# Attention, expert layer and feed-forward on one core: queries and keys laid nine tokens to a partition, second expert weights two rows to a partition

## The chip, the cores and the metric

One core of a Trainium2 chip runs the whole program in one launch. The metric is the device time of one execution in microseconds (us), the median of several executions.

## The reference, cut to what matters

Four batches of eight heads, 576 tokens, head size 64. Each head has a downsampled attention (means of four tokens) and a local one (tokens closer than four). The result, 2304 rows of 512, goes through a soft mixture of eight experts with four slots each and then through a feed-forward block with a squared relu.

```python
q_d = q.reshape(B, H, 144, 4, D).mean(axis=3)          # the same for k and v
out_up = np.repeat(sm_attn(q_d, k_d, v_d), 4, axis=2)
mask = np.abs(pos[:, None] - pos[None, :]) < 4
out_local = softmax(where(mask, q @ k.T / 8, -1e9)) @ v
x = (out_up + out_local) -> [2304, 512]
logits = x @ phi;  slot_input = softmax(logits, 0).T @ x
slot_out[e] = relu(slot_input[e] @ w1[e]) @ w2[e]      # 8 experts, 512 -> 1024 -> 512
y = softmax(logits, 1) @ slot_out
out = relu(y @ w_in) ** 2 @ w_out                      # 512 -> 2048 -> 512
```

## The kernel before, in words

The attention goes over 16 units, a unit being two heads of one batch (u = 0 to 15, four units a batch). The two heads lie on partitions 0 to 63 and 64 to 127 of most tiles. The order of all work is written out by hand: START for the first three units, then for every s from 3 to 15 the letters of ORDER, then DRAIN. Each letter is one function for one unit; in step s the letter T transposes unit s, S and s make the scores of unit s-1, p and q transpose the probabilities of unit s-2, and V, D, A and t make the values, their sum and the token rows of unit s-3. All engines take their instructions in that order.

Loads go through one queue, SP's, which issues them in the order of the program. A step loads queries and keys of unit s+2 (Q, `load_qk`, L343), two windowed loads of v for unit s-1 (L, `load_v`, L360, pieces of 64 numbers), v once more in groups of eight tokens for the downsampled path (4, `load_v4`, L374), and two or three pieces of 512 KB of the weights (l, `load_next`, L152, L155, L158; LOADN = [2, 2, 3] * 6 says how many, 2.33 on average). Queries and keys have two tiles each, so the load of unit s+2 waits for the transposes of unit s. The weight pieces lie in a ring of tiles that come free as the experts use them.

A load of queries or keys of a unit brings [2 heads, 576 tokens, 64]. Before the change a partition of 96 holds, for each head and each third of the tokens, two neighbouring tokens side by side, 128 numbers: six pieces of 512 B a partition. `transposes` (L377 to L392) turns it into [64 per head, tokens]: for each of q and k and each head, three transposes of [96, 128] into one PSUM tile "tr" [128, 3, 96] (L384). The even tokens then lie on its partitions 0 to 63 and the odd ones on 64 to 127, and two copies of 64x288 put them into every second column of `qs` or `kzs` (L390 ACT for q; L392 ACT for k of head 0, DVE for k of head 1). "tr" has three buffers in rotation, so the fourth group, k of head 1, waits for the two copies of the first.

What follows uses `qs` and `kzs` in token order: `downsample` on POOL (L400, L402), `scores_local` (L408, L414), `scores_down` (L438). `value_sums` (POOL, L482) and `value_sums2` (DVE, L488) add up v for the downsampled path, `values_down` (L523) multiplies with it. At the end of each batch `stage_g2` and `stage_g3` (L609 to L632) collect the slots' inputs.

The experts: `expert_up` (L824) multiplies with w1 into a tile with hidden columns 256g to 256g+255 on partitions 32g and up, `expert_mid` transposes that in two halves (L836), `expert_down` (L848) takes chunk by chunk of w2. A piece of w2 is [128, 2, 512], rows 256j + 128t + p before the change: two runs of 2 KB a partition. The feed-forward block (L909 to L1032) follows, 96 steps of nine 128x512 matmuls each.

Of the kernel before, what the change touches and what calls it, by code (L numbers as in the profile page):

```python
# [9 lines left out]
F32 = mybir.dt.float32  # L10
# [8 lines left out]
B, H, S, D = 4, 8, 576, 64  # L19
# [50 lines left out]
def attention_moe_ffn_kernel(  # L70
# [12 lines left out]
    nc = tc.nc  # L83
    cp = ctx.enter_context(tc.tile_pool(name="const", bufs=1))
    ring = ctx.enter_context(tc.tile_pool(name="ring", bufs=1))
# [5 lines left out]
    def bank(tag, shape, bufs, name, dt=F32):  # L91
        return ps.tile(shape, dt, tag=tag, bufs=bufs, name=name)

    def bt(shape, name):
        return bank("t", shape, 3, name)
# [4 lines left out]
    ident = cp.tile([128, 128], F32, name="ident")  # L100
# [5 lines left out]
    for g in range(4):  # L106
        r = slice(32 * g, 32 * g + 32)
# [34 lines left out]
    def load(kind, i, j, place):  # L142
        pool, tag = where[kind, i, j] = place
        name = f"{kind}{i}_{j}"
        if kind in ("win", "wout"):

            t = pool.tile([128, 512, 2], I32, tag=tag, name=name)
            if kind == "win":
                src = w_in.bitcast(I32).rearrange("(t p) f -> p t f", t=4)[:, i, 1024 * j:1024 * j + 1024]
            else:  # L150
                src = w_out.bitcast(I32)[128 * i:128 * i + 128]
            nc.sync.dma_start(out=t.rearrange("p f w -> p (f w)"), in_=src)  # L152
        elif kind == "w1":
            t = pool.tile([128, FE], F32, tag=tag, name=name)
            nc.sync.dma_start(out=t, in_=w1[i].rearrange("(p t) f -> p t f", t=4)[:, j])  # L155
        else:
            t = pool.tile([128, 2, DM], F32, tag=tag, name=name)
            nc.sync.dma_start(out=t, in_=w2[i].rearrange("(t p) f -> p t f", t=8)[:, 2 * j:2 * j + 2])  # L158
        got[kind, i, j] = t

    def load_next(n=1):
        for _ in range(n):
            if not loads or not free:
                return
            kind, i, j = loads[0]

            fits = [x for x in free if x[0] is not wa or kind in ("w1", "w2") and i == 0 and int(x[1][1:]) >= WRES]
            fits.sort(key=lambda x: x[0] is not wa)
            if kind == "wout" or kind == "win" and (LPOS[4 * j + i] > 50 or lb is None) or kind != "win" and i == NE - 1:
                fits = [x for x in free if x[0] is ring]  # L170
            elif kind != "win" and i >= LBE + 1:
                fits = [x for x in fits if x[1][0] != "b"]
                fits.sort(key=lambda x: x[0] is ring)

            if any(j > 1 and (j, i // 2) not in win for k, i, j in got if k == "win") and kind != "win":
                if sum(x[0] is ring for x in free) < 2:
                    fits = [x for x in fits if x[0] is not ring]
            if not fits:
                return
            place = fits[0]  # L180
            free.remove(place)
            loads.popleft()
            load(kind, i, j, place)
# [11 lines left out]
    for g in range(4):  # L195
        m = maskf[32 * g:32 * g + 32]
# [97 lines left out]
    with tc.tile_pool(name="att", bufs=1, side="right") as ap:  # L294
        NV = 2
        vws, qs, kzs = [], [], []
        for i in range(NV):

            t = ap.tile([128, NB, D], F32, name=f"vw{i}")
# [3 lines left out]
        for i in range(2):  # L303
            t = aq.tile([128, SP + 6], F32, name=f"q{i}")
# [4 lines left out]
            t = aq.tile([128, 2, SP + 6], F32, name=f"kz{i}")  # L309
# [25 lines left out]
        def load_qk(u):  # L335
            b, hp = divmod(u, NP)
            h0 = 2 * hp
            st = U[u]
            for nm, src in (("q", q), ("k", k)):

                t = ring.tile([128, 1024], F32, tag=f"{nm}{u % 2}", name=f"{nm}{u}")[0:96, 0:768]
                t = t.rearrange("p (h a c) -> p h a c", h=2, a=3)
                nc.sync.dma_start(out=t, in_=src[b, h0:h0 + 2].rearrange("h (a p r) d -> p h a (r d)", a=3, r=2))  # L343
                st[nm] = t

        def load_v(u):
# [30 lines left out]
        def transposes(u):  # L377
            st = U[u]
            for j, nm in enumerate("qk"):
                for h in range(2):  # L380

                    t = bt([128, 3, 96], f"tr{u}_{j}{h}")
                    for i in range(3):
                        nc.tensor.transpose(t[:, i], st[nm][:, h, i], ident[0:96, 0:96])  # L384
                    hr = slice(64 * h, 64 * h + 64)
                    to = (kzs[u % 2][hr, h] if j else qs[u % 2][hr])[:, 3:3 + S].rearrange("p (i c r) -> p i c r", i=3, r=2)
                    for r in range(2):
                        o, i_ = to[:, :, :, r], t[64 * r:64 * r + 64]
                        if not j:
                            nc.scalar.mul(out=o, in_=i_, mul=1.0 / 128.0)  # L390
                        else:
                            (nc.vector.tensor_copy if h else nc.scalar.copy)(out=o, in_=i_)  # L392
# [258 lines left out]
        def gate_rows(b):  # L651
# [6 lines left out]
            else:  # L658
# [8 lines left out]
                nc.vector.tensor_tensor(out=ctt_lo, in0=m, in1=ctt_hi, op=ALU.subtract)  # L667

        load_qk(0)
        for x in LOADS.split():  # L670
            if x[0] == "l":
                load_next(int(x[1:]))
            elif x == "phi":
                nc.sync.dma_start(out=phis, in_=phi.rearrange("(c p) s -> p c s", p=128))
            else:
                dict(Q=load_qk, L=load_v)[x[0]](int(x[1:])) if x[0] != "4" else load_v4(int(x[1:]))
# [3 lines left out]
        tm.enter_context(tc.manual_schedule())  # L680
        step = {
            "V": values, "T": transposes, "D": values_down, "A": value_adds, "Q": load_qk,
            "L": load_v, "S": scores_local, "p": probs_local, "E": exp_local, "s": scores_down, "d": downsample,
            "v": value_sums, "m": max_down, "q": probs_down, "e": exp_down, "n": norm_local, "N": norm_down,
# [52 lines left out]
        t = bt([1, 128], "mtp")  # L737
# [4 lines left out]
        t = bt([128, 2], "mbp")  # L742
# [23 lines left out]
        t = bt([128, 4, 32], "stp")  # L766
# [47 lines left out]
    for i in range(2):  # L814
        t = xp.tile([128, 2, 4, NS], F32, name=f"ht{i}")
# [3 lines left out]
    def expert_up(e):  # L819

        t = bank(("s", "sd")[e % 2], [128, 256], 1, f"hp{e}")
        for kt in range(4):
            for g in range(4):
                nc.tensor.matmul(  # L824
                    t[32 * g:32 * g + 32], sT[:, kt], got["w1", e, kt][:, 256 * g:256 * g + 256],
                    start=(kt == 0), stop=(kt == 3), tile_position=(0, 32 * g), skip_group_check=True,
                )
            done("w1", e, kt)
        hs = xp.tile([128, 256], F32, tag="hs", bufs=2, name=f"hs{e}")
        nc.scalar.activation(out=hs, in_=t, func=AF.Relu)  # L830
        return hs

    def expert_mid(e, hs):
        t = bt([128, 2, 4, NS], f"htp{e}")
        for i in range(2):
            nc.tensor.transpose(t[:, i].rearrange("p g s -> p (g s)"), hs[:, 128 * i:128 * i + 128], ident)  # L836

        ht = hts[e % 2]
        if e >= 2:
            nc.gpsimd.memset(ht[:, :, :, 4 * e - 8:4 * e - 4], 0.0)  # L840
        nc.scalar.copy(out=ht[:, :, :, 4 * e:4 * e + 4], in_=t[:, :, :, 4 * e:4 * e + 4])
        return ht
# [20 lines left out]
    hs = expert_up(0)  # L863
    for e in range(NE):
        if e == 0:
            hs, hs1 = expert_up(1), hs
            ht = expert_mid(0, hs1)
        else:
            ht = expert_mid(e, hs)
            if e + 1 < NE:  # L870
                hs = expert_up(e + 1)
# [165 lines left out]
    for i in range(2, len(steps) + LOOK):  # L1037
        up = lambda name, shape: pf.tile(shape, F32, tag="up", bufs=2, name=name)
        for x in SLOTS.get(i, ()):
            j = int(x[1:])  # L1040
# [6 lines left out]
        if i < len(steps):  # L1047
            c, f = steps[i]
# [43 lines left out]
```

## Time and profile before

| | us |
|---|---|
| three timed executions | 459.60, 465.48, 466.72 |
| their median | 465.48 |
| span of the profiled execution | 462.2 |

The span is from the first to the last instruction in one execution, 3.3 us less than the median of the timed ones; a time of its own is not recorded for the profiled execution. It falls into attention (to about 185 us), experts (to about 223), and the feed-forward block. PE is TensorE, with PEld its weight loads; DVE, ACT, POOL and SP are the other engines; PEclk and "clock" are the granted TensorE clock as a share of 2.4 GHz (0.5 is 1.2 GHz). The rows of the trace stand in a section of their own below.

### The profile page before, as it was taken

What the parts mean: (1) busy time and instruction counts of PE and PEld (TensorE: products, weight loads), DVE (VectorE), ACT (ScalarE), POOL (GpSimd) and SP (SyncE); (2) the same over time, 40 slices, a digit from 0 to 9 for tenths busy, and PEclk for the clock granted to TensorE, in tenths of its full rate; (3) what the DMA queues carried; (4) which work ended last, traced back from release to release, by engine and by line L of the source; (5) the groups of instructions that cost most, each with busy time, mean ns of one, the idle gap of its engine ahead of it and who ended that gap; (6) DMA issues with size and microseconds to landing.
All of it is one profiled execution on the core that took longest, in us unless ns stands there. A gap on an engine that the chain in (4) does not pass through costs nothing.

```text
span 462.2 us, 10525 instructions
## 1 busy us (share of the span) xinstructions
PE 422.8 (91%) x4098; PEld 324.1 (70%) x4098; DVE 286.0 (62%) x608; ACT 265.5 (57%) x665; POOL 116.7 (25%) x173
## 2 busy tenths in 40 slices
PE   5589999878979979999989999999999999999996
PEld 4367776665767656455557887888888888888885
DVE  4367686656978963142299999946456545556442
ACT  4458887756667542124598898875444445444442
POOL 5248766756757850002000000000000000000000
PEclk9769999987988989799999999999999999999999
DMA  9979999999999986999996000003001001001001
GB/s 180 216 275 239 233 260 245 258 235 210 250 223 251 241 268 226 390 398 389 408 409 277 1 1 0 2 0 138 0 0 69 0 1 69 0 2 69 1 0 68
DMA packets 63851, 75.19 MB, mean 163 GB/s; under 512 B 24250, under 2 KB 42938, under 8 KB 63802
## 3 DMA queue, kind: packets, MB, share of 16 engines
q1 hardware_dynamic: 63658, 74.39, 57.9%
q8 instruction: 32, 0.52, 0.5%
q14 instruction: 17, 0.14, 0.1%
q10 hardware_dynamic: 144, 0.13, 0.1%
HBM read 69.79 MB, written 4.72 MB: 161 GB/s over the span
## 4 chain that ended last, share of the span: by engine, by line
PE 63%; DMA 11%; DVE 9%; ACT 9%; SPq 4%; issue 2%; POOL 2%; POOLq 0%; DVEq 0%; ACTq 0%
PE po L1016 38%; DMA vw<-in_v_dram 6%; PE hp L824 4%; DMA v<-in_v_dram 4%; PE so L848 3%; PE up L956 3%; PE av L510 2%; SPq L360 2%; ACT q L390 2%; SPq L374 2%; PE ptp L476 1%; DMA q<-in_q_dram 1%; PE pdp L497 1%; PE sd L438 1%; ACT pd L449 1%
## 5 line engine op out<-in xcount | busy, mean ns | idle before, releaser
L1016 PE MATMUL po<-wparts,ghi 128*128 128x512 f32 x576 | 149.0, 392 | 2.3 <-DVE wparts L914 2.3
L1016 PEld LDWEIGHTS po<-wparts,ghi 128*128 128x128 f32 x576 | 106.7, 188 | 23.8 <-DVE wparts L914 3.7
L961 ACT ACTIVATE r<-up 128x384 f32<-128x384 f32 x96 | 46.9, 489 | 72.8 <-PE up L956 68.0
L1016 PE MATMUL po<-wparts,glo 128*128 128x512 f32 x288 | 81.6, 390 | 0.5 <-DVE glo L969 0.5
L965 DVE TENSOR_TENSOR r<-r 128x384 f32<-128x384 f32 x64 | 35.6, 556 | 58.6 <-ACT ghi L964 58.6
L1016 PEld LDWEIGHTS po<-wparts,glo 128*128 128x128 f32 x288 | 53.9, 188 | 12.3 <-DVE glo L969 1.1
L969 DVE TENSOR_TENSOR glo<-r,ghi 128x384 fp32r<-128x384 f32 x94 | 52.3, 556 | 13.6 <-ACT ghi L968 7.4
L964 ACT ACTIVATE ghi<-r 128x384 fp32r<-128x384 f32 x66 | 34.7, 526 | 2.1
L956 PE MATMUL up<-cst,ast 128*128 128x384 f32 x96 | 33.0, 345 | 0.7 <-DVE ast L947 0.4
L390 ACT ACTIVATE q<-tr 64x288 f32<-64x288 f32 x64 | 27.4, 429 | 10.3 <-PE tr L384 9.4
L462 POOL TENSOR_TENSOR pl<-elp,sm 64x350 f32<-64x350 f32 x30 | 28.5, 950 | 12.9 <-DVE sm L460 7.0
L482 POOL TENSOR_TENSOR v<-v 72x512 f32<-72x512 f32 x16 | 21.2, 1327 | 27.5 <-DMA v<-in_v_dram 27.5
L392 DVE COPY kz<-tr 64x288 f32<-64x288 f32 x32 | 14.7, 458 | 19.0 <-PE tr L384 18.6
L510 PEld LDWEIGHTS av<-pt,vw 64*64 64x64 f32 x640 | 21.8, 145 | 3.2 <-issue 3.0
L510 PE MATMUL av<-pt,vw 64*64 64x58 f32 x640 | 23.9, 230 | 0.0
L384 PE MATMUL tr<-ident,k 96*128 96x96 f32 x96 | 16.2, 290 | 7.5 <-ACT q L390 7.4
L956 PEld LDWEIGHTS up<-cst,ast 128*128 128x128 f32 x96 | 17.9, 188 | 5.2 <-DVE ast L947 0.7
L384 PE MATMUL tr<-ident,q 96*128 96x96 f32 x96 | 13.4, 285 | 8.8 <-POOL maskf L198 4.6
L477 ACT COPY pt<-ptp 128x512 f32<-128x512 f32 (+1 forms) x32 | 12.1, 429 | 16.4 <-PE ptp L476 16.3
L488 DVE TENSOR_TENSOR vd<-v 72x256 f32<-72x256 f32 x16 | 11.4, 711 | 15.6 <-POOL v L482 15.6
L400 POOL TENSOR_TENSOR s<-kz 64x288 f32<-64x288 f32 x30 | 20.3, 678 | 2.3
L476 PE MATMUL ptp<-ident,pl 128*128 128x128 f32 x80 | 14.9, 324 | 6.3 <-POOL pl L462 3.8
(188 smaller groups left out, 692.6 us busy)
## 6 DMA issues: line engine op xcount, KB each, us to landing
w<-in_moe_w_dram SPq DMA_DIRECT2D x64, 512.0 KB, 9.1
win<-in_moe_w_in_dram SPq DMA_DIRECT2D x16, 512.0 KB, 9.4
wout<-in_moe_w_out_dram SPq DMA_DIRECT2D x16, 512.0 KB, 10.8
vw<-in_v_dram SPq DMA_DIRECT2D x30, 160.0 KB, 5.6
q<-in_q_dram SPq DMA_DIRECT2D x16, 288.0 KB, 8.8
k<-in_k_dram SPq DMA_DIRECT2D x16, 288.0 KB, 6.3
out_dram<-o SPq DMA_DIRECT2D x17, 256.0 KB, 2.2
v<-in_v_dram SPq DMA_DIRECT2D x16, 256.0 KB
```

What stands on the lines that cost most here:

```text
L384: nc.tensor.transpose(t[:, i], st[nm][:, h, i], ident[0:96, 0:96])
L390: nc.scalar.mul(out=o, in_=i_, mul=1.0 / 128.0)
L400: eng.tensor_tensor(out=s1[r], in0=t[:, :, 0], in1=t[:, :, 1], op=ALU.add)
L462: (nc.vector if u in NDVE else nc.gpsimd).tensor_tensor(out=pl[r, :, c0:c0 + W], in0=el[r], in1=sm[r, 0:NB].unsqueeze(2).to_broadcast([64, ...
L482: nc.gpsimd.tensor_tensor(out=v4[:, :, 0], in0=v4[:, :, 0], in1=v4[:, :, 1], op=ALU.add)
L510: nc.tensor.matmul(av[a][rr, 2 * HQ * i:2 * HQ * i + 2 * HQ].rearrange("p (f c) -> p f c", f=2), vw[rr, 2 * i + a], ptv[rr, i, :, a, 0:HQ] ...
L956: nc.tensor.matmul(t, ast[:, 128 * f:128 * f + 128], cst[:, c * n:c * n + n], start=True, stop=True)
L961: nc.scalar.activation(out=r, in_=t, func=AF.Relu)
L964: nc.scalar.activation(out=ghi, in_=r, func=AF.Square)
L965: nc.vector.tensor_tensor(out=g, in0=r, in1=r, op=ALU.mult)
L969: nc.vector.tensor_tensor(out=glo, in0=g, in1=ghi, op=ALU.subtract)
L1016: nc.tensor.matmul(po[c][i], a[:, 128 * i:128 * i + 128], w[f], start=(f == 0 and w is whi and a is ghi), stop=(f == NF - 1 and a is glo), ...
```

## The change

Queries and keys: a unit's tile is now [128, 576]: partition 64h + p holds tokens 9p to 9p+8 of head h, one run of 2304 B. Each head is transposed from its own 64 partitions, 128 columns (two tokens) at a time: four transposes of [64, 128] and one of [64, 64] for the ninth token. "tr" is [128, 5, 64]; the first token of each pair lies on partitions 0 to 63 (five chunks), the second on 64 to 127 (four chunks). The two copies bring 64x320 and 64x256 numbers, reading across the chunks so that the columns of `qs` and `kzs` stay in token order.

w2: a piece's rows are 256j + 2p + t, so a partition reads one run of 4 KB; `expert_mid` takes every second hidden column to match.

```diff
-            nc.sync.dma_start(out=t, in_=w2[i].rearrange("(t p) f -> p t f", t=8)[:, 2 * j:2 * j + 2])
+            nc.sync.dma_start(out=t, in_=w2[i].rearrange("(j p t) f -> p j t f", j=4, t=2)[:, j])
...
-                t = ring.tile([128, 1024], F32, tag=f"{nm}{u % 2}", name=f"{nm}{u}")[0:96, 0:768]
-                t = t.rearrange("p (h a c) -> p h a c", h=2, a=3)
-                nc.sync.dma_start(out=t, in_=src[b, h0:h0 + 2].rearrange("h (a p r) d -> p h a (r d)", a=3, r=2))
+                t = ring.tile([128, 1024], F32, tag=f"{nm}{u % 2}", name=f"{nm}{u}")[:, 0:9 * D]
+                nc.sync.dma_start(out=t, in_=src[b, h0:h0 + 2].rearrange("h (p r) d -> (h p) (r d)", r=9))
...
-                    t = bt([128, 3, 96], f"tr{u}_{j}{h}")
-                    for i in range(3):
-                        nc.tensor.transpose(t[:, i], st[nm][:, h, i], ident[0:96, 0:96])
+                    t = bt([128, 5, 64], f"tr{u}_{j}{h}")
                     hr = slice(64 * h, 64 * h + 64)
-                    to = (kzs[u % 2][hr, h] if j else qs[u % 2][hr])[:, 3:3 + S].rearrange("p (i c r) -> p i c r", i=3, r=2)
+                    for i in range(5):
+                        m = min(128, 9 * D - 128 * i)
+                        nc.tensor.transpose(t[0:m, i], st[nm][hr, 128 * i:128 * i + m], ident[hr, hr])
+                    to = (kzs[u % 2][hr, h] if j else qs[u % 2][hr])[:, 3:3 + S].rearrange("p (c r) -> p c r", r=9)
                     for r in range(2):
-                        o, i_ = to[:, :, :, r], t[64 * r:64 * r + 64]
+                        o, i_ = to[:, :, r:9:2], t[64 * r:64 * r + 64, 0:5 - r].rearrange("p i c -> p c i")
...
-            nc.tensor.transpose(t[:, i].rearrange("p g s -> p (g s)"), hs[:, 128 * i:128 * i + 128], ident)
+            nc.tensor.transpose(t[:, i].rearrange("p g s -> p (g s)"), hs[:, i:256:2], ident)
```

The order of the work stays; what stands in it changes its form. On PE, step 3 of the attention, between the values of unit 0 (av) and the scores of unit 2 (s), the kernel before has four groups of three transposes (tr_00 and tr_01 are q of heads 0 and 1, tr_10 and tr_11 are k):

```order
L510 MATMUL av_1_423<-pt,vw_130 64x58 x10
L523 MATMUL av_0_422<-pdt_385,vd_404 64x144 x4
L384 MATMUL tr_00_449<-ident,q_248 128x96 x3
L384 MATMUL tr_01_455<-ident,q_248 128x96 x3
L384 MATMUL tr_10_461<-ident,k_250 128x96 x3
L384 MATMUL tr_11_467<-ident,k_250 128x96 x3
L408 LDWEIGHTS identb
L408 MATMUL s_485<-maskb,identb 128x350
L414 MATMUL s_485<-kz_139,q_136 29x70 x20
```

The changed kernel has, at the same place on PE:

```order
L523 MATMUL av_0_446<-pdt_409,vd_428 64x144 x4
L385 MATMUL tr_00_473<-ident,q_264 128x64 x4
L385 MATMUL tr_00_473<-ident,q_264 64x64
L385 MATMUL tr_01_481<-ident,q_264 128x64 x4
L385 MATMUL tr_01_481<-ident,q_264 64x64
L385 MATMUL tr_10_489<-ident,k_266 128x64 x4
L385 MATMUL tr_10_489<-ident,k_266 64x64
L385 MATMUL tr_11_497<-ident,k_266 128x64 x4
L385 MATMUL tr_11_497<-ident,k_266 64x64
L408 LDWEIGHTS identb
L408 MATMUL s_517<-maskb,identb 128x350
L414 MATMUL s_517<-kz_139,q_136 29x70 x20
```

Twelve transposes of 96 moving columns a unit have become twenty of 64; nothing has changed places with them.

On ACT the copies out of "tr" in the same step stand in the kernel before between the value sums of unit 0 (xd) and the probabilities of unit 1 (pt):

```order
L528 ACTIVATE xd<-av_0_422 128x288
L390 ACTIVATE q_141<-tr_00_449 64x288 x2
L390 ACTIVATE q_141<-tr_01_455 64x288 x2
L392 COPY kz_144<-tr_10_461 64x288 x2
L477 COPY pt<-ptp_0_511 128x512
```

And in the changed kernel:

```order
L528 ACTIVATE xd<-av_0_446 128x288
L390 ACTIVATE q_141<-tr_00_473 64x64x5
L390 ACTIVATE q_141<-tr_00_473 64x64x4
L390 ACTIVATE q_141<-tr_01_481 64x64x5
L390 ACTIVATE q_141<-tr_01_481 64x64x4
L392 COPY kz_144<-tr_10_489 64x64x5
L392 COPY kz_144<-tr_10_489 64x64x4
L477 COPY pt<-ptp_0_543 128x512
```

There are as many copies as before, in the same place, now of 64 runs of five or four numbers each.

## Rows read from the trace of the kernel before

**Rows 1.** The page: DMA engines' busy share and rate in 40 slices.

```profile
DMA  9979999999999986999996000003001001001001
GB/s 180 216 275 239 233 260 245 258 235 210 250 223 251 241 268 226 390 398 389 408 409 277 1 1 0 2 0 138 0 0 69 0 1 69 0 2 69 1 0 68
```

**Rows 2.** The chain that ended last, in order of time, 59 to 104 us.

```profile
59.42 9.11 DMA vw<-in_v_dram
...
96.35 5.60 DMA v<-in_v_dram
...
102.08 1.27 POOL v L482
```

**Rows 3.** PE's timeline: start, length, line, operation; the wait before it in brackets.

```profile
17.01 1.20 PE L384 MATMUL tr<-ident,q 96*128 96x96 f32 x6 [4.21 <-DMA q<-in_q_dram]
...
33.10 0.81 PE L414 MATMUL s<-kz,q 128*29 128x70 f32 x40
...
57.60 0.81 PE L414 MATMUL s<-kz,q 128*29 128x70 f32 x40
...
69.49 1.07 PE L622 MATMUL sip<-xk,ee 128*32 128x512 f32 x8
...
71.54 0.47 PE L554 MATMUL lgt<-xt,phis 128*32 128x128 f32 x16
...
104.31 0.71 PE L523 MATMUL av<-pdt,vd 72*64 72x144 f32 x8 [1.59 <-DVE vd L488]
...
160.53 0.81 PE L414 MATMUL s<-kz,q 128*29 128x70 f32 x40
```

**Rows 4.** Stretches of the span: busy time of each engine, clock, DMA share, rate.

```profile
core 0: us, PE busy (x) PEld busy (x) DVE busy (x) ACT busy (x) POOL busy (x), PEclk, DMA share, GB/s
17.00:31.10 14.10, 11.51 (x126) 8.96 (x126) 7.98 (x19) 7.09 (x23) 2.69 (x2) 0.53 0.91 294
31.10:57.60 26.50, 24.68 (x451) 19.58 (x449) 17.02 (x41) 21.84 (x65) 21.97 (x30) 1.00 0.97 218
57.60:160.50 102.90, 90.40 (x1480) 67.82 (x1479) 77.42 (x159) 68.92 (x216) 71.64 (x91) 0.92 1.11 243
185.30:223.00 37.70, 37.11 (x518) 18.42 (x522) 9.14 (x36) 10.43 (x38) 3.44 (x12) 0.93 1.04 395
```

**Rows 5.** Who waited for whom, 57.6 to 160.5 us: total, times, longest.

```profile
POOL v L482 <- DMA v<-in_v_dram: 25.3, 9, 4.4
DVE vd L488 <- POOL v L482: 14.5, 7, 3.2
```

**Rows 6.** The page: DMA packets by size, and issues: count, KB, us to landing.

```profile
DMA packets 63851, 75.19 MB, mean 163 GB/s; under 512 B 24250, under 2 KB 42938, under 8 KB 63802
...
vw<-in_v_dram SPq DMA_DIRECT2D x30, 160.0 KB, 5.6
```

**Rows 7.** PE's timeline, transposes of one unit, and a later matmul of 64 columns.

```profile
39.29 0.71 PE L384 MATMUL tr<-ident,q 96*128 96x96 f32 x6
39.84 0.41 PE L384 MATMUL tr<-ident,k 96*128 96x96 f32 x3
40.71 0.47 PE L384 MATMUL tr<-ident,k 96*128 96x96 f32 x3 [0.45 <-ACT q L390]
...
226.62 0.55 PE L925 MATMUL sotp<-sel,sos 128*128 128x64 f32 x4
```

**Rows 8.** One line's instructions: ns of one, least, median, most.

```profile
L384 PE MATMUL tr<-ident,q x96: 246/246/422, 4.6 to 148.1; 96*128 96x96 f32 x96
```

**Rows 9.** Groups by line: busy us, mean ns of one, idle before it.

```profile
L390 ACT ACTIVATE q<-tr 64x288 f32<-64x288 f32 x64 | 27.4, 429 | 10.3 <-PE tr L384 9.4
L392 DVE COPY kz<-tr 64x288 f32<-64x288 f32 x32 | 14.7, 458 | 19.0 <-PE tr L384 18.6
L536 DVE TENSOR_TENSOR xt<-av,xd 128x290 f32<-128x290 f32 x32 | 13.2, 454 | 4.0 <-PE xrp L566 3.6
...
L925 PE MATMUL sotp<-sel,sos 128*128 128x64 f32 x4 | 0.6, 260 | 0.0
```

## Prediction

> **What bounds the kernel now.** I read the page's slices first. The DMA engines are busy nine tenths or more in nearly every slice until about 250 us, yet they move 210 to 275 GB/s during attention and 390 to 409 GB/s with the experts [rows 1]. So in attention the engines are full without moving much. Then the chain of waits: from 59 us on it runs through loads of v, up to the POOL addition that waits for them [rows 2]. The table of waits agrees: POOL waits 25.3 us in nine places for v, DVE 14.5 us for POOL behind it [rows 5].
>
> PE's timeline says what that costs. Units 2 to 5 start their local scores at 33.10 to 57.60 us, (57.60 - 33.10) / 3 = 8.17 us a unit at clock 1.00 [rows 3, 4]. There PE sets the pace, with 24.68 of 26.50 us busy [rows 4]. From there ten units to 160.53 take 102.9 us. At 8.17 they would take 81.7, and the collection of the slots, 71.54 - 69.49 = 2.05 us, comes three times in it, 6.2: together 87.9. So 15.0 us are lost, part of it directly (as in the wait of 1.59 us at 104.31), part because the clock falls after such waits: its mean over the stretch is 0.92 [rows 3, 4]. In the start PE waits 4.21 us for the queries of unit 2, and then runs 14.1 us at clock 0.53 [rows 3, 4]. With the experts PE is busy 37.11 of 37.70 us [rows 4], so loads don't bound it there, however full their queue is.
>
> **The change, part by part.** *Queries and keys, DMA.* A unit's two loads are 2 x 576 pieces of 512 B before, 2 x 128 pieces of 2304 B after: 18,432 - 4,096 = 14,336 packets fewer over 16 units. Their bytes, 2 x 288 KB = 0.59 MB a unit, stay. What is a packet worth? Over the slow stretch a unit has 102.9 / 10 = 10.29 us, at 243 GB/s [rows 4] 2.5 MB. Of these, v in groups of eight (288 KB) and 2.33 pieces of 512 KB make 1.52 MB in pieces of 2 KB or more, at the experts' 395 GB/s [rows 4] 3.84 us. The remaining 6.45 us go to 1,152 pieces of 512 B and v's two windowed loads of 160 KB, 1,280 pieces of 256 B [rows 6]. Shared by number, queries and keys take 1,152 / 2,432 of that, 3.05 us; afterwards 0.59 MB at 395 GB/s, 1.49 us: 1.56 us saved. That is one end. At the other, the large pieces are slowed just as much by the company of v's small ones; then 0.59 MB takes 0.59 / 0.243 = 2.4 us either way and nothing is saved. I take 1.0 us, nearer to the count, since the rate differs most between stretches with and without small pieces. So DMA needs 9.3 us a unit, 93 us for ten.
>
> The Trainium skill, "DMA: Bandwidth & Descriptors" (Specifications), puts the least size for line rate at 512 B; by it these pieces run at full rate already and nothing is saved. The trace can't separate the two sizes, but does show that the mix of 256 and 512 B runs far below the experts' rate; the rule is the first rival below.
>
> *Transposes.* Three of 96 columns take 0.41 us and two groups of them 0.71; one takes 0.246, so (0.41 - 0.246) / 2 = 0.08 us lies between two [rows 7, 8]. After the change there are five of 64 columns in each group. If the spacing goes with the columns, it is 0.08 x 64 / 96 = 0.055 us. If a weight load of 128 columns sets it, the nearest row is the matmul of 64 columns at 226.62, (0.55 - 0.26) / 3 = 0.097 [rows 7, 9]. I take 0.06, since transposes with weights of 128 columns already come 0.08 apart. Two groups of a unit lie on the path: the first, whose copies free the buffer for the fourth, and the fourth; the other two fill the wait of 0.45 us between [rows 7]. Each grows from 2 x 0.08 to 4 x 0.06, so a unit grows by 2 x 0.08 = 0.15 us (0.1 to 0.45). For the ten units of the slow stretch PE then needs 87.9 + 1.5 = 89.4 us, less than DMA's 93. The other six pay 0.9 us (0.6 to 2.7).
>
> The skill's "TensorE: Matmul & The Clock Gate" (LDWEIGHTS) has a weight load last columns / 1.2 ns, 107 ns for 128 columns. By that the twelve transposes of before could not come 0.08 us apart, which they do [rows 7], so I set it aside; with it a unit would grow by 16 x 107 + 4 x 53 - 12 x 107 = 640 ns, 10 us over 16 units, an estimate.
>
> *Copies.* Six on 64x288, 429 ns on ACT and 458 on DVE [rows 9], become pairs of 64x320 and 64x256: the same sum. They now go through PSUM across chunks, in runs of five or four. The nearest row for short runs is the value addition, 290 numbers in runs of two in 454 ns, no dearer than the plain 458 [rows 9]. I take nothing. Price if wrong: the third rival.
>
> *w2.* 32 loads have 256 packets of 2 KB, then 128 of 4 KB. With the experts PE hides it all, so nothing; the half microsecond by which PE is not busy there [rows 4] is the most it could give, and a loss would need loads to fall behind PE.
>
> *The sum.* In the slow stretch the larger need decides, DMA's 93 us, and I leave 1 us for waits that remain: 102.9 - 94 = 8.9 us gained (0 to 13.5, the latter if PE's 89.4 decides). In the start the first loads of queries and keys and the issues behind them get shorter; I count 3 of the 4.21 us, and 1 for the clock, since a shorter wait may leave it high. The bounds are 0 and 4.2 plus half of PE's 11.51 us at half clock, about 10. Minus 0.9 for the other units: 8.9 + 4 - 0.9 = 12.0. The drain, the experts and the feed-forward block move earlier as they are, since each is bound by its own engines. 462.2 - 12.0 = 450.2 in the profiled span; the timed median is 3.3 above that span, so 453.5.
>
> **Rivals.** *First: 512 B was no worse than 2304 B.* What is slow would be v's 256 B alone, and queries and keys would only change shape. For it: half the small packets and both named waits are v's [rows 5, 6]. Against it: in the start, where queries and keys are about half of the load, the rate is lowest, 180 GB/s [rows 1]. The transposes' growth hides in the waits of the slow stretch, the other units pay 0.9 to 2.7: 466 to 468.
>
> *Second: the relief is half spent.* DMA's need stays so near to PE's that a single late v still stops PE for a microsecond and the clock falls again. For it: the clock at 0.92 shows how a few waits cost a whole stretch [rows 4]. It would give 4 us there and 2 in the start, minus 0.9: 460.
>
> *Third, slower: the copies across chunks.* If ACT and DVE pay for each jump between chunks, PE feels it in the fourth group, which waits for both copies of the first, and ACT in six copies a unit. ACT has 21.84 / 26.50 x 8.17 = 6.7 us of work in an undisturbed unit [rows 4]. If a copy doubles (+0.43), ACT needs 9.3 us a unit, about what a unit takes now without the collections, (160.53 - 33.10 - 6.2) / 13 = 9.3; from there on it decides. At +0.6 us a copy it is 10.3 us, 13 more over 13 units, less 3 of the start: about 476. Against it: the row on runs of two [rows 9].
>
> **How the numbers follow.** The forecast has 0.62 and, from its bounds, its own range 444 to 458; the first rival 0.13, the second 0.17, the third 0.08. A measurement of this kernel can tell about 2%, 9.3 us, from no change: faster means below 456.2, slower above 474.8. Of the forecast 0.57 lies below 456.2 and 0.05 above. So faster 0.57; same 0.05 + 0.12 + 0.17 + 0.01 = 0.35; slower 0.01 + 0.07 = 0.08. The range that holds 8 in 10 runs from 445 to 466: below it the best of the start and PE's bound together, above it the third rival and the worse end of the first.
>
> **What would show it.** Right: packets fall by 14,336 and 4,096 to about 45,400; the rate in the slices of attention rises towards 260 to 290 GB/s; POOL's 25.3 us for v fall to a third or less; local scores follow each other by 8.3 to 8.6 us at a clock near 1; experts start at about 173 instead of 185 us, and all behind them is as long as before. A spacing of transposes near 0.06 and copies near 450 and 405 ns on ACT confirm those terms. Wrong: waits for v unchanged with fewer packets (first rival), few waits but a clock still near 0.92 (second), copies above 0.8 us (third), or an expert phase that now waits for weights, which would mean that its loads were bound by DMA after all.

## The result, and the profile after

The changed kernel takes 457.94 us in the median of 19 executions, the kernel before, run beside it, 464.79. The ratio is 0.9884 with a 95% interval from 0.9851 to 0.9917: 1.2% faster, where 2.6% was forecast. Medians are over all executions, while this ratio and those below leave out executions over 1.5% above the fastest of their kernel, so a ratio is not the quotient of two medians. The profiled execution has a span of 456.4 us, 1.8 less than its own time of 458.17.

On the page of the changed kernel the lines that answer to [rows 1] and [rows 6] are:

```profile
DMA  8889998999997549999992000003001001001001
GB/s 192 238 291 250 307 286 215 258 255 281 284 257 222 164 170 345 411 407 408 408 410 103 1 1 0 2 0 140 0 0 70 0 1 70 0 2 70 1 0 69
DMA packets 45420, 75.20 MB, mean 165 GB/s; under 512 B 24250, under 2 KB 24506, under 8 KB 45370
...
vw<-in_v_dram SPq DMA_DIRECT2D x30, 160.0 KB, 4.8
```

The packets have fallen to 45,420 as forecast. The mean rate of the first 13 slices has risen from 237 to 257 GB/s, and at the end of attention (the 14th to 16th slice, 148 to 183 us) the DMA engines now have time to spare. The same stretches of the span as in [rows 4], the last moved with the experts:

```profile
core 0: us, PE busy (x) PEld busy (x) DVE busy (x) ACT busy (x) POOL busy (x), PEclk, DMA share, GB/s
17.00:31.10 14.10, 10.85 (x140) 8.02 (x140) 8.21 (x20) 8.22 (x27) 3.79 (x4) 0.64 0.83 272
31.10:57.60 26.50, 24.54 (x509) 19.77 (x510) 19.55 (x44) 21.59 (x64) 22.69 (x31) 1.00 1.00 275
57.60:160.50 102.90, 90.32 (x1633) 68.33 (x1631) 81.83 (x168) 71.68 (x224) 71.33 (x91) 0.97 0.96 248
178.90:216.60 37.70, 37.33 (x510) 19.00 (x510) 9.13 (x36) 10.34 (x38) 3.46 (x12) 0.93 1.03 409
```

The table of waits, 57.6 to 160.5 us, answers to [rows 5]:

```profile
POOL pl L462 <- ACT xk L564: 14.2, 8, 5.8
ACT elp L428 <- DVE elp L423: 12.4, 10, 3.3
...
PE tr L385 <- ACT q L390: 8.1, 9, 2.1
...
POOL v L482 <- DMA v<-in_v_dram: 6.0, 5, 1.8
```

POOL's wait for v has fallen from 25.3 to 6.0 us. Other waits stand above it now, and none of them is for a load. In the slow stretch itself, though, the rate has hardly moved, 248 GB/s for 243. PE's timeline, as in [rows 3]:

```profile
15.66 0.61 PE L385 MATMUL tr<-ident,q 64*128 64x64 f32 x10 [1.62 <-DMA q<-in_q_dram]
...
31.15 0.81 PE L414 MATMUL s<-kz,q 128*29 128x70 f32 x40
...
55.97 0.81 PE L414 MATMUL s<-kz,q 128*29 128x70 f32 x40
...
101.49 0.51 PE L385 MATMUL tr<-ident,k 64*128 64x64 f32 x5 [1.21 <-ACT q L390]
102.47 1.39 PE L414 MATMUL s<-kz,q 128*29 128x70 f32 x40
...
153.03 0.81 PE L414 MATMUL s<-kz,q 128*29 128x70 f32 x40
159.81 0.71 PE L523 MATMUL av<-pdt,vd 72*64 72x144 f32 x8 [1.95 <-DVE vd L488]
...
178.93 0.66 PE L824 MATMUL hp<-w,sT 128*32 128x256 f32 x4 [0.38 <-DVE sT L771]
```

In the kernel before, the experts began at 185.35 us:

```profile
185.35 1.08 PE L824 MATMUL hp<-w,sT 128*32 128x256 f32 x8 [0.38 <-DVE sT L771]
```

An undisturbed unit takes (55.97 - 31.15) / 3 = 8.27 us, 0.10 more than before. The ten units after that take 153.03 - 55.97 = 97.1 us where they took 102.9. Matmuls of the same form take 1.39 us behind the wait of 1.21 us, against 0.81: the granted clock from 102.4 to 103.9 us is 0.50, which is 1.2 GHz. The 5.8 us of span come to: 2.0 in the start (33.10 against 31.15), -0.3 in three undisturbed units, 5.9 in the slow stretch, -1.1 in the drain (24.8 us before, 178.93 - 153.03 = 25.9 now) and -0.7 behind it.

These are single traces, and how far two of them differ can be seen from the runs below. The ten units take 101.8 to 103.3 us in five kernels with the 96 partitions of before and 96.8 to 98.0 in three with the changed loads and the rest of attention as in the changed kernel (but for two loads that change places in one), so the gain there is clear of the spread. The scores of unit 2 start between 30.9 and 33.1 us in those five, and between 29.8 and 32.8 in all that load onto 128 partitions; the drain lasts 24.8 to 25.8 us in the five. Neither the 2.0 us of the start nor the 1.1 us of the drain is clear of the spread.

The groups of the new transposes and copies:

```profile
L385 PE MATMUL tr<-ident,k 64*128 64x64 f32 x128 | 15.1, 243 | 11.8 <-ACT q L390 11.7
L390 ACT ACTIVATE q<-tr 64x320 f32<-64x320 f32 x32 | 14.3, 448 | 7.0 <-PE tr L385 6.4
...
L390 ACT ACTIVATE q<-tr 64x256 f32<-64x256 f32 x32 | 13.7, 428 | 0.4
```

The two copies of a head on ACT take 448 + 428 = 876 ns, 2 x 429 = 858 before [rows 9]. The transposes of one unit, the last three of the third group and the five of the fourth:

```profile
46.01 0.34 PE L385 MATMUL tr<-ident,k 64*128 64x64 f32 x3
47.00 0.51 PE L385 MATMUL tr<-ident,k 64*128 64x64 f32 x5 [0.65 <-ACT q L390]
```

### The profile page after: what moved, and what is told of

Its sections match the earlier page's. It is cut to its first block, busy times and chain, and to the rows that moved or that the text cites. A ratio compares the mean times of both kernels' runs of the same rounds, so it can differ in the third digit from the quotient of the medians.

```text
span 456.4 us, 10781 instructions
## 1 busy us (share of the span) xinstructions
PE 420.4 (92%) x4226; PEld 322.3 (71%) x4226; DVE 288.5 (63%) x608; ACT 266.7 (58%) x665; POOL 115.8 (25%) x173
## 2 busy tenths in 40 slices
DMA packets 45420, 75.20 MB, mean 165 GB/s; under 512 B 24250, under 2 KB 24506, under 8 KB 45370
## 4 chain that ended last, share of the span: by engine, by line
PE 66%; DVE 16%; ACT 12%; DMA 2%; issue 2%; SPq 1%; POOL 1%; DVEq 0%; ACTq 0%; POOLq 0%
PE po L1016 39%; PE hp L824 4%; PE so L848 3%; PE up L956 3%; ACT pd L449 3%; PE av L510 2%; ACT q L390 2%; DVE xt L536 2%; DVE win L215 2%; DVE kz L392 2%; PE ptp L476 2%; PE sd L438 2%; DMA vw<-in_v_dram 1%; PE tr L385 1%; PE pdp L497 1%
## 5 line engine op out<-in xcount | busy, mean ns | idle before, releaser
L390 ACT ACTIVATE q<-tr 64x320 f32<-64x320 f32 x64 | 28.0, 438 | 7.4 <-PE tr L385 6.4
L462 POOL TENSOR_TENSOR pl<-elp,sm 64x350 f32<-64x350 f32 x30 | 25.8, 859 | 23.6 <-ACT xk L564 15.5
L385 PE MATMUL tr<-ident,k 64*128 64x64 f32 (+1 forms) x160 | 17.1, 241 | 11.8 <-ACT q L390 11.7
L392 DVE COPY kz<-tr 64x320 f32<-64x320 f32 (+1 forms) x32 | 14.7, 460 | 18.0 <-PE tr L385 17.7
L482 POOL TENSOR_TENSOR v<-v 72x512 f32<-72x512 f32 x16 | 22.3, 1397 | 6.2 <-DMA v<-in_v_dram 6.2
L385 PEld LDWEIGHTS tr<-ident,k 64*128 64x128 f32 (+1 forms) x160 | 12.4, 144 | 14.7 <-ACT q L390 14.4
L449 ACT ACTIVATE pd<-sd,mx 128x144 f32<-128x144 f32 x48 | 18.4, 383 | 1.6 <-DVE mx L442 0.6
```

The costliest lines, as they stand in the source:

```text
L385: nc.tensor.transpose(t[0:m, i], st[nm][hr, 128 * i:128 * i + m], ident[hr, hr])
L449: nc.scalar.activation(out=pd[:, t], in_=sd[:, t], func=AF.Exp, bias=mx[:, 10 + t:11 + t], accum_out=ss[:, t:t + 1],)
L462: (nc.vector if u in NDVE else nc.gpsimd).tensor_tensor(out=pl[r, :, c0:c0 + W], in0=el[r], in1=sm[r, 0:NB].unsqueeze(2).to_broadcast([64, ...
```

## The experiments

The first question was what ends last in the slow stretch now. Two theories: DVE, whose chain holds the narrowing of w_in (A), or loads still (B). Narrowing is the work that makes 32-bit numbers of the 64-bit w_in for the feed-forward block, in turns spread over attention. Two views speak against B. The first is the chain that ended last, by engine, in the kernel before and in the changed one: DMA's share of the span falls from 11% to 2%, DVE's rises from 9% to 16%.

```profile
PE 63%; DMA 11%; DVE 9%; ACT 9%; SPq 4%; issue 2%; POOL 2%; POOLq 0%; DVEq 0%; ACTq 0%
PE 66%; DVE 16%; ACT 12%; DMA 2%; issue 2%; SPq 1%; POOL 1%; DVEq 0%; ACTq 0%; POOLq 0%
```

The second is what the queue of loads waited for from 57.6 to 160.5 us. Loads of queries and keys (`load_qk`) wait 0.9 us for PE's transposes to free their tiles before the change and 21.8 us after it: they now run ahead of PE.

```profile
SPq L343 <- PE tr L384: 0.9, 2, 0.6
...
SPq L342 <- PE tr L385: 21.8, 12, 4.8
```

In the chain of the changed kernel, from 119 to 125 us it is DVE almost throughout, with the narrowing (win) in front of the copies of keys and the value sums:

```profile
118.97 0.45 ACT pd L449 x2
...
119.65 0.24 DVE sm L460
119.89 1.20 DVE win L212 x2
121.08 1.97 DVE win L215 x2
...
123.06 0.49 DVE kz L392
...
124.03 0.83 DVE xt L536 x2
124.85 0.44 DVE mx L422
```

**Light narrowing, on the changed kernel and on the one before.**

```diff
             yield two(out=di, in0=hi, scalar1=0x7FFFFFFF, scalar2=None, op0=ALU.bitwise_and)
+            c = slice(0, 16)
+            hi, lo, dst, di = hi[:, c], lo[:, c], dst[:, c], di[:, c]
```

> The changed kernel, with all narrowing steps but the first on 16 instead of 512 columns as long as attention runs (the first steps' full width keeps order, loads and waits; the values of w_in are not those of the reference). It takes some 20 us of DVE work out of attention and no load. Theory A, DVE's chain with the narrowing in it has taken the place of DMA in the slow stretch: the ten units from score start 5 to 15 shrink from 97.1 us to 89 to 91 (8.28 a unit and three collections of 2.05), experts start near 171 instead of 178.9, the time falls by 6 to 8 us to about 450 to 452. Theory B, DMA still sets the pace there and the relief was simply smaller than forecast: the ten units stay within 1.5 us of 97 and the time within 2 us of 457.9.

> The kernel before with the same reduced narrowing during attention (the values of w_in are not those of the reference). Theory A: there the loads ended last, so taking DVE work away gives little: the ten units stay at 100 us or more (102.9 before), POOL still waits 20 us or more for v, the time falls by 0 to 3 us from 464.8. Theory B, and the view that DVE's work costs both kernels the same: it falls by as much as in the changed kernel, the one that DVE holds by 6 to 8 us.

Measured: 453.44 us on the changed kernel (ratio to the kernel before 0.980, 0.967 to 0.993), its ten units 151.02 - 56.42 = 94.6 us, POOL's wait for v 10.1 us. On the kernel before 459.38 (0.996, 0.991 to 1.001), POOL's wait 20.4 us, and PE's timeline there:

```profile
58.14 0.82 PE L416 MATMUL s<-kz,q 128*29 128x70 f32 x40
...
157.73 0.81 PE L416 MATMUL s<-kz,q 128*29 128x70 f32 x40
```

Its ten units take 157.73 - 58.14 = 99.6 us, 3.3 less than with the full narrowing; on the changed kernel it is 2.5 less. The drain shrinks alike, by 3.2 us before (179.35 - 157.73 = 21.6 against 24.8) and by 3.1 in the changed kernel (173.78 - 151.02 = 22.8 against 25.9). So the traces don't bear out what A expected, that DVE's work costs the changed kernel and hardly the one before: DVE's narrowing costs both about the same, and the two ratios are too wide to tell them apart. Nor is it enough, for 2.5 us of the stretch are far from all of the 8 that were missing (97.1 against 89). The longer waits for v in the changed kernel with DVE out of the way say that loads are close behind.

**No loads of v in groups of eight; and both taken away.**

```diff
         def load_v4(u):
+            if u >= 2:
+                U[u]["v4"] = U[u % 2]["v4"]
+                return
```

> The changed kernel without the loads of v in groups of eight from the third unit on; the tiles of the first two units are used again, so the downsampled values are not those of the reference. It takes away the load that POOL waits for and 288 KB a unit. If loads still hold the slow stretch, its ten units fall from 97.1 us to 91 or less; if DVE holds it, to no less than 95.

> Both taken away from the changed kernel: narrowing on 16 columns during attention and no loads of v in groups of eight from the third unit on (neither the values of w_in nor the downsampled values are those of the reference). If DVE's narrowing and those loads are the only things between the stretch and PE's own pace, the ten units take 89 to 90 us at clock 1.00. If something else falls in, a wait of another engine or a clock that falls without a late load, they take 93 us or more.

Measured: without the loads 456.0 us in the median of two (0.984, 0.974 to 0.995), ten units 152.63 - 57.34 = 95.3 us; with both taken away 448.47 (0.968, 0.958 to 0.978), ten units 148.98 - 55.12 = 93.9 us. So these loads are worth 1.8 us of the stretch and DVE's narrowing 2.5, together 3.2 (each from one trace, with the spread named above), and 93.9 is not 89: something is left that neither theory had. PE's timeline of the run with both taken away shows it at the end of a batch:

```profile
99.31 0.51 PE L390 MATMUL tr<-ident,k 64*128 64x64 f32 x5 [1.74 <-ACT q L395]
```

and ACT's timeline, before the copies of queries that this waits for:

```profile
97.38 0.38 ACT L596 ACTIVATE ee<-lgt,nm 128x144 f32<-128x144 f32 x1 [0.97 <-DVE nm L595]
...
97.75 0.28 ACT L604 ACTIVATE al<-mb,nm 128x1 f32<-128x1 f32 x1
97.94 0.25 ACT L581 COPY lsb<-lgt 128x128 f32<-128x128 f32 x1
98.08 0.42 ACT L533 ACTIVATE xd<-av 128x288 f32<-128x288 f32 x1
98.38 1.79 ACT L395 ACTIVATE q<-tr 64x320 f32<-64x320 f32 x4
```

At a batch's end ACT waits for DVE's maxima, takes the slots' exponentials and keeps the logits, and only then copies the next unit's queries. PE waits 1.74 us for these copies, and the granted clock from 101 to 104 us, behind the wait, is 0.53.

**The end of a batch moved.** `stage_g1` now takes the maxima alone and `stage_g1c` the rest. The exponentials and copies come after the next unit's value additions, the transposes of them after the next scores, into a buffer of the rotation instead of the one of the downsampled scores.

```diff
-ORDER = "VDTAQL4gSpsEvdmqwenGtNlc"
+ORDER = "VDTAQL4SpgsEvdmqwenGtNlc"
...
-                    stage_g1(b)
-                    stage_g1b(b)
-                    keep_logits(b)
+                    stage_g1(b)
...
+                    if x == "A" and last(u4):
+                        stage_g1c(u4 // NP)
+                        stage_g1b(u4 // NP)
+                        keep_logits(u4 // NP)
...
-            t = bank("sd", [128, 2, 128], 1, f"etp{b}")
+            t = bt([128, 2, 128], f"etp{b}")
```

> The run without v's loads in groups of eight and with light narrowing (values as left out there), and the work at the end of a batch moved: the exponentials of the slots' logits and the copies that keep them come on ACT and DVE after the next unit's copies of queries and keys, not before, and the transposes of these exponentials come after the next scores. If what is left there (93.9 us for ten units instead of 89) is PE waiting for ACT at the ends of batches and the clock that falls behind it, the ten units fall to 89 to 91 us and PE's wait before the fourth group of transposes stays under 0.8 us in every unit. If it is something else, they stay at 93 or more.

Measured: 445.02 us in the median of two (0.958, 0.949 to 0.968), and PE's timeline:

```profile
55.03 0.81 PE L419 MATMUL s<-kz,q 128*29 128x70 f32 x40
...
98.61 0.51 PE L390 MATMUL tr<-ident,k 64*128 64x64 f32 x5 [0.65 <-ACT q L395]
...
145.25 0.81 PE L419 MATMUL s<-kz,q 128*29 128x70 f32 x40
```

Ten units in 90.2 us, and the wait at the same place is 0.65 us as in any other unit. The granted clock over the ten units is 1.00, where it was 0.96 without the move. The remaining 3.7 us were the ends of batches and the clock behind them.

**What made the loads lighter.** The forecast counted packets. This run brings the changed kernel's layout in nearly as many packets as before:

```diff
-                nc.sync.dma_start(out=t, in_=src[b, h0:h0 + 2].rearrange("h (p r) d -> (h p) (r d)", r=9))
+                sv = src[b, h0:h0 + 2].rearrange("h (p r) d -> (h p) (r d)", r=9)
+                nc.sync.dma_start(out=t[:, 0:4, 0:128], in_=sv[:, 0:512].rearrange("p (i c) -> p i c", i=4))
+                nc.sync.dma_start(out=t[:, 4, 0:64], in_=sv[:, 512:576])
...
```

> The changed kernel with queries and keys laid out as it has them, nine tokens on each of 128 partitions and the same transposes and copies, but each partition's run brought in four pieces of 512 B and one of 256 B, by two loads: 640 packets a tensor and unit, against 128 in the changed kernel and 576 before. Theory A, the number of packets is what gave the gain: the ten units take 102 us or more again, POOL waits 20 us or more for v, the time is 464 to 469, as before or somewhat slower. Rival C, it is the spread over 128 instead of 96 partitions that made the loads faster: it stays near the changed kernel, 457 to 460.

Measured: 458.35 us (0.995, 0.990 to 1.001), ten units 155.63 - 57.65 = 98.0 us, POOL's wait for v 13.8 us. The stretch is as short as in the run with queries and keys alone further down (98.0), with 62,316 packets in all. So the number of packets is not what mattered most. The ratio alone couldn't show it, since its interval reaches 1.000. Three runs on the kernel before, with its 96 partitions, its transposes and copies, change the loads alone:

```diff
-                t = t.rearrange("p (h a c) -> p h a c", h=2, a=3)
-                nc.sync.dma_start(out=t, in_=src[b, h0:h0 + 2].rearrange("h (a p r) d -> p h a (r d)", a=3, r=2))
+                t = t.rearrange("p (h a c) -> p h a c", h=2, a=3)[:, :, :, 0:128]
+                for h in range(2):
+                    nc.sync.dma_start(out=t[:, h], in_=src[b, h0 + h].rearrange("(p a r) d -> p a (r d)", a=3, r=2))
```

This is the run with neighbouring pieces, in a tile with a gap behind each piece; without the gap it is the run with long pieces, and without the gap and with "(a p r)" in the last line the control.

> The kernel before, its transposes and copies untouched, but the loads of queries and keys bring each partition's three pieces of 512 B of a head from next to each other in memory (one load a head, a gap of 64 B in the tile). The tokens then come in another order than the copies take them for, so the scores are not the reference's; packets, bytes and all work stay. If the neighbourhood of the pieces made loads lighter, POOL's waits for v fall from 25 us to under 15 and the ten units from 102.9 to 100 or less; if only 128 partitions or long runs do that, they stay at 102 to 104.

> The control for the run before this one: the kernel before with one load a head, the pieces 49 KB apart in memory as they were. Splitting a load in two changes nothing in its packets: the ten units stay at 102 to 104 us, the time at 463 to 467. If the split itself helps or harms, it shows here.

> The kernel before with the same order of tokens as in the run with neighbouring pieces, but without the gap, so that a partition's 1536 B of a head are one packet: 192 a tensor instead of 576, still on 96 partitions (scores again not the reference's, all work untouched). If fewer packets count beyond their neighbourhood, the ten units are 1 us or more shorter than with neighbouring pieces; if 128 partitions are what counts, they stay at 102 or more.

Measured, with the mean time of a packet of queries and keys between 57.6 and 140 us, worked out from the traces' packet records (POOL's wait from 57.6 to 160.5):

```
layout                               ten units  POOL for v  packet      ns   B/ns
before, 96 partitions, 49 KB apart     102.9       25.3      512 B     45.2  11.3
the same in two loads                  101.8       20.8      512 B     42.3  12.1
96 partitions, neighbours              102.2       19.9      512 B     43.1  11.9
96 partitions, long                    103.3       23.8     1536 B    107.3  14.3
128 partitions, in pieces               98.0       13.8      512 B     29.3  17.5
128 partitions, one run (changed)       97.1        6.0     2304 B    116.2  19.8
```

The trace with neighbours is of an execution of 463.41 us, close to that kernel's median. Neighbourhood does nothing that can be seen (43.1 against 42.3 ns), three times longer packets on 96 partitions shorten neither the waits for v nor the stretch, and the same 512 B take 29 ns on 128 partitions. The times go the same way in their medians, 463.68, 462.10 and 461.53 us with neighbours, control and long pieces against 458.35 in pieces on 128 partitions, but the ratios don't separate the layouts: 0.992 (0.984 to 1.000), 0.998 (0.994 to 1.002) and 0.994 (0.990 to 0.998) against 0.995. So the reading rests on the stretch, the waits and the packets. By these, what the loads gained they gained mostly by the 128 partitions. Long runs there show in POOL's wait, in the packets and in the wait of `load_qk` for PE's transposes (21.8 us against 5.2 in pieces), not in the stretch, where 98.0 and 97.1 are within the spread. The run in pieces on 128 partitions also has the changed transposes and copies. No run has these with loads onto 96 partitions; that they don't shorten the stretch by themselves is argued from the undisturbed unit, which they lengthen. Why 96 partitions are slower these runs don't say.

**The two parts alone.** The kernel before with the new w2, and the changed kernel with the old w2; the edits are the lines of the change.

> The kernel before with the second expert weights alone changed to two rows a partition. Theory A: PE hides these loads, so nothing beyond the interval, 464 to 465.5. Rival D, halving these 8192 packets relieves the full queue in the second half of attention too: 2 to 4 us faster than before, 461 to 463.

> The changed kernel with the second expert weights as before the change: queries and keys alone. If w2 is hidden, 456.5 to 459, as the changed kernel, and with it all of the gain; if w2 gave part of it, 460 to 462.

Measured: w2 alone 466.60 us in the median of four (1.011, 0.993 to 1.030), ten units 102.3 us, no difference that can be seen; queries and keys alone 455.44 (0.981, 0.974 to 0.989), ten units 98.0 us, all of the gain. Loads of w2 stay behind PE.

**Order changes on the changed kernel.** The first swaps two loads, the second also moves narrowing turns to the experts' phase, the third adds the moved end of a batch, as above.

```diff
-ORDER = "VDTAQL4gSpsEvdmqwenGtNlc"
+ORDER = "VDTAQ4LgSpsEvdmqwenGtNlc"
...
-CONV = {3: 1, 4: 1, 5: 1, 6: 1, 7: 1, 8: 2, 9: 1, 10: 0, 11: 2, 12: 2, 13: 2, 14: 1, 15: 3}
+CONV = {3: 1, 4: 1, 5: 1, 6: 1, 7: 1, 8: 2, 9: 1, 10: 0, 11: 2, 12: 2, 13: 1, 14: 0, 15: 1}
-NEXP = {(2, 0): 1}
+NEXP = {(0, 0): 1, (1, 0): 1, (2, 0): 1, (3, 0): 1, (4, 0): 1}
```

> The changed kernel with one swap in the order of a step: v in groups of eight is loaded before the windowed loads of v, since it is needed a step earlier. If what is left of the wait for loads still counts in the changed kernel, POOL's 6.0 us for v fall below 2, the wait of 1.95 us before the values of the downsampled path near the end goes, and the time falls by 1 to 3 us from 457.9. If DVE alone sets the pace of the slow stretch, the time stays within 1 us.

> The same swap, and the last narrowing turns (seven DVE pairs of steps 13 to 15 and after) put off to the experts' phase, where DVE is busy for a quarter of the time. If DVE's narrowing late in attention is what was added to the path, experts start 2 to 4 us earlier than in the run with the swap alone and the time is 452 to 455; if the experts' phase pays for it, or the steps wait for something else, the time stays where the swap alone has it.

> The changed kernel, complete, with three changes of order: v in groups of eight loaded first, the last narrowing turns in the experts' phase, and the end of a batch moved as in the run before this one. If batch ends are a cost beside DVE and the loads, 1 to 4 us better than the two other changes together: 451 to 454. If DVE holds the same steps anyway, 455 as there.

Measured: the swap alone 458.31 us (0.994, 0.990 to 0.999), ten units 96.8, no gain beside the changed kernel; with the narrowing moved 455.04 (0.983, 0.974 to 0.993), experts at 176.24 us instead of 177.85, ten units 95.2 us; all three 453.16 (0.976, 0.969 to 0.982), ten units 147.34 - 54.50 = 92.8 us.

```profile
54.50 0.81 PE L414 MATMUL s<-kz,q 128*29 128x70 f32 x40
...
147.34 0.81 PE L414 MATMUL s<-kz,q 128*29 128x70 f32 x40
```

The last beats both kernels. In this complete kernel the moved end of a batch brings 2.3 us of the stretch (95.18 to 92.84). That the swap takes POOL's wait for v away and the time stays says that this wait did not set the pace. Whether these changes of order would bring as much on the kernel before was not run.

**Six tokens on 96 partitions.** Long runs with the three plain transposes of before, columns of `qs` and `kzs` in token order; and the same in pieces.

```diff
+                nc.sync.dma_start(out=t, in_=src[b, h0:h0 + 2].rearrange("h (p r) d -> p h (r d)", r=6))
...
+                    to = (kzs[u % 2][hr, h] if j else qs[u % 2][hr])[:, 3:3 + S].rearrange("p (c i r) -> p i c r", i=3, r=2)
```

> The changed kernel with six tokens of a head on each of 96 partitions: two runs of 1536 B a partition, 192 packets a tensor, and the three transposes of 96 columns and plain copies of before. Units undisturbed take 8.17 us again instead of 8.28. If long runs are what counts, loads are as light as in the changed kernel and the time is 455 to 458; if the spread over 128 partitions is what counts, POOL's waits for v come back (over 12 us) and the time is 459 to 463.

> The same six tokens on 96 partitions, but brought in pieces of 512 B (a gap of 64 B in the tile between them, one load a head): 576 packets a tensor as before the change, now with the three pieces of a partition next to each other in memory. If the neighbourhood of the pieces made the difference between before and the run with small pieces on 128 partitions, POOL waits 8 to 16 us for v and the ten units take 97 to 99 us; if the 128 partitions made it, POOL waits over 20 us and they take 101 or more.

Measured: 474.60 us (1.022, 1.015 to 1.030) and 472.98 (1.019, 1.009 to 1.028), both slower than either kernel, for a reason that no expectation had. The group of ACT's copies in the first of them:

```profile
L390 ACT ACTIVATE q<-tr 64x288 f32<-64x288 f32 x64 | 44.1, 688 | 6.7 <-PE tr L385 5.9
```

The same 288 numbers take 688 ns, not 429, when they are written 24 B apart instead of 8. An undisturbed unit takes (63.18 - 34.14) / 3 = 9.68 us, and POOL waits for v only 2.5 us and 1.9 us. So the stretch says nothing on loads in these two. The packets do a little: in the second a piece of 512 B took 35.4 ns between 57.6 and 140 us, less than the 43.1 of the same loads in the run with neighbouring pieces, so a packet's time is no fixed price of a layout; yet it is still more than the 29.3 on 128 partitions.

## Why the prediction was wrong

The direction held, and the first half of the mechanism: loads of queries and keys got lighter, POOL's waits for v went from 25.3 to 6.0 us, and the time fell. The size did not: 5.8 us of span for 12.0.

*The slow stretch* is the main miss, 5.9 us gained for 8.9. The step that failed is "In the slow stretch the larger need decides, DMA's 93 us, and I leave 1 us for waits that remain". DMA's need did not decide: the run with all three changes of order has every load and does the ten units in 92.8 us, and without v's loads in groups of eight the stretch is only 1.8 us shorter. And the waits that remain are not 1 us: in the prediction's own sum they came out as 97.1 - 93 = 4.1. Of the 97.1 us, the run with everything taken away leaves 90.2, so 6.9 us remain above PE's pace: 3.7 at the ends of batches, which stand in the prediction with PE's collection of the slots alone and not with the wait for ACT before it, and 3.2 for DVE's narrowing and v's loads together. PE's own need, forecast as 89.4, came out near the 90.2.

Behind this stands a reading of the kernel before: all of the 15.0 us above PE's pace were put down to late loads and the clock behind them. Light narrowing takes 3.3 us of the same stretch there, with POOL still waiting 20.4 us for v, so part of it never was the loads' alone. How the two are tied in that kernel no run shows. The busy share of the DMA engines, from which the prediction read that they bound attention, doesn't tell: over the ten units it is 0.97 in the changed kernel and 1.02 in the one that takes 92.8 us.

"DMA needs 9.3 us a unit" was on the safe side, by luck: 1,152 packets of 45 ns on 16 engines are 3.25 us, 256 of 116 ns 1.86, so by this estimate 1.4 us a unit were saved where I took 1.0. The second rival was nearer in size (460 us), "the relief is half spent", but had a wrong cause: the waits for ACT and the work of DVE held PE, and the swap that took POOL's wait for v away brought no time. The mean clock is 0.97 after 0.92; what the clock cost beside the waits no run separates. The offset of 3.3 us between span and time mixed two executions: within one execution it is 1.8 us here.

*What made the loads lighter* was also wrong in the working: I shared the time by the number of packets, and the 128 partitions did most of it. The first rival's result, no gain, did not come. Of its ground, the 512 B that the Trainium skill ("DMA: Bandwidth & Descriptors", Specifications) puts as the least size for line rate, the packets show both sides: on 128 partitions 512 B moved 17.5 B/ns, near the 19.8 of 2304 B, and on 96 partitions 11.3.

*The start* gave 2.0 us for 4, a difference within the spread of the traces. PE's wait for queries fell from 4.21 to 1.62 us as thought, but the clock was low all the same: 14.1 us at 0.64 instead of 0.53.

*The transposes* came out right: with 0.22 us for one, the last three of the third group lie (0.34 - 0.22) / 2 = 0.06 us apart and the five of the fourth (0.51 - 0.22) / 4 = 0.07, and a unit grew by 0.10 where I had 0.15. The Trainium skill's formula for a weight load ("TensorE: Matmul & The Clock Gate", LDWEIGHTS) gives 107 ns for 128 columns, an estimate; it does not set the spacing of these transposes, which is 60 to 70 ns. *The copies* across chunks cost 18 ns a pair, as good as the nothing I took. *w2* is nothing, as forecast. *The drain* I moved as it was. It grew by 1.1 us, within the spread, and light narrowing shortens it by 3.1 us here and by 3.2 in the kernel before: DVE's narrowing is on its path in both.

## What to carry to other kernels

When a late load is taken away, the stage does not fall to the busiest engine's undisturbed pace. Before a whole loss is put down to loads, take work from another engine in the kernel as it is: here DVE's narrowing was worth 3.3 us while loads were still late. Measure the pace over a whole period with its rare parts (here the end of a batch), not over its quiet units. To see whether loads end last, read what their queue waits for, not the busy share of the DMA engines. Spread a load over all 128 partitions before counting its packets. Where an order is written by hand, a faster stage asks for the order to be made anew: three changes of order gave as much again as the change itself.

## What the runs showed of the hardware that was not expected

Loads of 512 B pieces took 42 to 45 ns each on 96 partitions (35 in a slower stage) and 29 ns on 128 in much the same mix of loads; pieces of 1536 B on 96 partitions took 107 ns, so that they moved 14 B/ns against 20 for 2304 B on 128. From 57.6 to 160.5 us the DMA engines showed a busy share of 0.96 while the queue that issues loads waited 21.8 us for PE. A copy of 288 numbers from PSUM costs 429 ns on ACT when it writes them 8 B apart and 688 ns at 24 B apart, and on DVE 458 and 692, while a pair of copies in runs of four or five numbers 8 B apart costs as much as the plain pair (876 ns against 858 on ACT).
